# Attention followed by a gated FFT convolution on one core: a rewritten order of the first two batches, one hand-over per group of filter spectra, and output rows in fewer, larger transfers

## Chip, cores and metric

The kernel runs on one NeuronCore of a Trainium2 chip. The metric is the device time of one execution in microseconds. A run's span is the time from the first to the last instruction in the profile; the execution's own time is a little longer than its span.

## What is computed

Eight batches of 576 rows. A linear attention without softmax gives x (eight heads of 64 columns, side by side: 512 columns), and a gated long convolution follows:

```python
kv  = einsum('bhsd,bhse->bhde', k, v)
out = einsum('bhsd,bhde->bhse', q, kv)
x   = out / sqrt(mean(out*out, axis=-1) + 1e-6) * g_norm      # heads side by side
x1, x2, x3 = split(x @ w_proj, 3, axis=-1)
X2  = rfft(x2, n=576, axis=1);  H = rfft(filter_fft, n=576, axis=0)
y   = x1 * irfft(X2 * H, n=576, axis=1) * x3
result = y @ w_out                                             # (8, 576, 512), fp32
```

## The kernel before

All work is written as named steps, and three strings, FIRST, ROUND and LAST, give the order in which the steps are written. `do(words, r)` walks a string: a word stands for a step of batch r, each `+` adds one to the batch, each `-` takes one off. A step that was done already, or whose batch doesn't exist, is skipped. FIRST holds the set-up and most of the first two batches, ROUND is walked for r = 0 to 6, LAST closes batch 7. Nothing reorders the instructions later: each engine runs its own in the order written, and waits on semaphores for the others.

The steps of a batch are these. Lk, Lv and Lq load k, v and q; POOL issues them and they are turned into bf16 on the way (line 100). K makes the eight k-v products (line 313) and eK copies them to `kvblk`. Qt transposes q by a transfer that SP issues (line 333); for batches 0 and 1, T0 and T1 do it on PE (line 340). O multiplies (line 376); sq (ACT, line 386) squares; R sums the squares through a matrix of ones, `ind` (line 383); rs takes the reciprocal root (ACT, line 397); ob or ov scales by g_norm; x0 and x1 multiply (DVE, line 409), which completes x. The transform is done in matmuls. 576 = 3 x 192, so fr, fd and fa (DVE, lines 420 to 434) fold x into a sum and two differences with mirrored halves; rrM, rrT, abM and abT multiply the folded parts by the middle third of w_proj (lines 450 to 471); err, eab and eT bring them to bf16 (ACT, line 475); F0, F1 and F2 apply the tables of cosines. M0, M1 and M2 multiply by the filter's spectra (DVE, lines 511, 512, 527), A0 (POOL) and Av1 (DVE) add the products (line 518). Ga and Gb are the gates from the first and last third of w_proj (line 537), x1j and gj their evacuations (lines 543, 545). Io and I transform back (lines 561, 562), os, u, w and fin put the rows together and gate them (`yg`, line 582). U0, U2 and U4 are the output product (line 609), ot0, ot2 and ot4 copy it to an `ot` tile and send it out from SP. Batch 7 uses V0 to V3 (line 641) with smaller pieces, whose copies run on ACT (va) and DVE (vv).

The set-up: Z and Zi fill constants (Zi's identity and counters on POOL), Zt and An0 to An2 make the angles and `IV`, the table for the inverse transform; Act asks ACT for the table set with the reciprocal root. Tb0 to Tb2 transpose `IV` into the forward tables, Ff0 to Ff2 fold the filter (line 261), and H0 to H2 make its spectra `HH` and `HM`: six or twelve matmuls, then for each half an ACT copy with a scale (line 289) and a DVE step (line 290). Words such as W1_ put four matmuls on zeros (W0_: ten, line 79) in front of the next step that takes a PSUM buffer.

PSUM is four pairs of banks. `take` gives the pair that was freed longest ago in the written order, so the order also decides who waits for whom. `ot` tiles are three, taken in turn:

```python
def ot_tile():
    turn[0] += 1
    return buf("ot", turn[0] % 3, [P, 2, DM], FP32)
```

Row order: column block `blk` of 32 holds the rows t, t + 6, t + 12 and so on, with t = `t_of(blk)`, so a block of 32 goes out with a step of six rows. U0 and U2 send pairs of such blocks, four transfers of 128 KB each; U4 and each V send four transfers of 64 KB, one for each block (lines 629 and 648). V's transfers go half from SP and half from ACT (va) or POOL (vv).

The transfers issued by SP and ACT take eight semaphores in turn, and a transfer waits until the one that last used its semaphore has landed.

Of the kernel before, what the change touches and what calls it, by code (L numbers as in the profile page):

```python
# [9 lines left out]
FP32 = mybir.dt.float32  # L10
BF16 = mybir.dt.bfloat16
I32 = mybir.dt.int32
AF = mybir.ActivationFunctionType
# [3 lines left out]
MAGIC = 3.0 * (2.0 ** 22)  # L17


FIRST = """Z Lq Lf Zi Lka Act Zt Lva An0 An1 An2 Lvb W0_ T1 Zf T0 eTv0 eTv1 Tb0 Lkb Lq+ Lw2 Ff2 Ff0 Tb2 Ff1 W2_ Ka eKa W1_ Tb1 O1 sq1  # L20
ov1 O0 sq0 R0 rs0 W6_ R1 Kb eKb rs1 ov0 O2 sq2 ov2 W7_ O3 Lk+ R2 sq3 R3 rs2 x0 rs3 ov3 x1 Lv+ fr1 T0+ fr0 T1+ eTa0+
Lw1 eTa1+ H2 H0 rrM fd0 rrT fa0 fd1 err fa1 W8_ H1 F0 W9_ abM eab K+ M0 eK+ abT O2+ eT sq2+ O0+ F2 sq0+ F1 ob2+ Lw3
ob0+ O3+ M2 sq3+ Lwo ob3+ M1 R2+ Ga0 Lq++ rs2+ Ga1 R3+ R0+ x10 Gb0 x11 O1+ A0 Av1 rs3+ rs0+ g0 Gb1 sq1+ ob1+
Lk++ R1+ x1+ Ga3 Ga2 g1 Io01 rs1+ Gb3 x13 Lv++ x0+ fr+ x12 os01 I01 rrM+ rrT+ fd+ fa+ g3 err+ abT+ eT+ Io23
u01 os23 I23 abM+ F0+ eab+ Gb2 F2+ u23 M0+ F1+ g2 M1+ w23 fin23 w01 fin01 K++ Lk+++ Qt++ Lq+++ eK++ W12_ O2++"""

ROUND = """K++ Lk+++ x0+ Qt++ U0- Lq+++ x13 eK++ fd+ Io23 u01 O2++ fa+ Gb3 fr+ ot0- Lv+++ os23 I23 abM+ g3 sq2++ u23
ob2++ rrM+ eab+ abT+ rrT+ eT+ U4- O1++ w01 err+ ot4- sq1++ ob1++ O3++ sq3++ fin01 ob3++ F1+ U2- w23 fin23 F0+
ot2- M1+ Ga1+ x11+ F2+ Ga0+ M0+ Gb0+ x10+ A0+ R3++ M2+ O0++ Gb1+ g0+ R2++ rs3++ Ga2+ g1+ sq0++ Av1+ ob0++
rs2++ R0++ x1++ Gb2+ x12+ R1++ rs0++ rs1++ g2+ Ga3+ Io01+ os01+ I01+"""  # L30

LAST = """u01 Io23 x13 U0- I23 w01 U2- os23 u23 fin01 ot0- Gb3 w23 ot2- g3 fin23 V2 V1 U4 va2 vv1 V3 V0 ot4 vv3 va0"""


@with_exitstack
def kernel(
# [19 lines left out]
    NB = S // 32  # L56
# [4 lines left out]
    act, vec = nc.scalar, nc.vector  # L61
# [71 lines left out]
    step = {}  # L133
# [135 lines left out]
    def gen_h(g):  # L269
        ff = tmp['ff']  # L270
        hp = take("h")
        n = N1 if g == 0 else P
        for ri in range(2):
            for a in range(3):
                m = P if a < 2 else 32
                kw = dict(start=(a == 0), stop=(a == 2))
                if g < 2:
                    nc.tensor.matmul(hp[:n, ri], FW[:m, a, 2 * g + ri, 0:n], ff[:m, a, ri], **kw)
                else:
                    for dup in range(2):  # L280
                        nc.tensor.matmul(hp[dup * NM:(dup + 1) * NM, ri], FW[:m, a, 4 + ri, ri * NM:(ri + 1) * NM], ff[:m, a, ri], **kw)
        u = work.tile([P, 2, DM], FP32, name="hu", tag="ot%d" % g)
        if g < 2:
            todo = [(HH[:n, g, 1], 0, cf[:n, 0, g:g + 1], cf[:n, 1, g:g + 1]),
                    (HH[:n, g, 0], 1, cf[:n, 0, g:g + 1], cf[:n, 2, g:g + 1])]
        else:
            todo = [(HM[:, i], 0, pc[:, 2 * i:2 * i + 1], pc[:, 2 * i + 1:2 * i + 2]) for i in range(2)]
        for i, (o_, ri, c1, c2) in enumerate(todo):
            act.activation(out=u[:n, i], in_=hp[:n, ri], func=AF.Copy, scale=c1)
            vec.scalar_tensor_tensor(out=o_, in0=hp[:n, 1 - ri], scalar=c2, in1=u[:n, i], op0=ALU.mult, op1=ALU.add)  # L290
        free("h")
        if g < 2:
            act.activation(out=HH[:n, g, 2], in_=HH[:n, g, 0], func=AF.Copy, scale=-1.0)

    for g in range(3):
        step["H%d" % g] = lambda b, g=g: gen_h(g)
    for n_, (d_, s_) in dict(Lw1=(wp[:, :, 0:DM], moe_w_proj[:, 0:DM]), Lw2=(wp[:, :, DM:2 * DM], moe_w_proj[:, DM:2 * DM]),
                             Lw3=(wp[:, :, 2 * DM:D3], moe_w_proj[:, 2 * DM:D3]), Lwo=(wo, moe_w_out)).items():
# [62 lines left out]
    sq = lambda: buf("sq", 0, [P, NDC, S])  # L361
    osb = lambda: buf("o", 0, [P, NDC, S])
    rstd = lambda: buf("rstd", 0, [P, NDC, S])
# [229 lines left out]
    def o_rows(b, *blks):  # L593
        t0 = [t_of(x) for x in blks]
        two = [[(t0[1] - t0[0]) * DM, 2]] if len(t0) == 2 else []
        return bass.AP(tensor=out.tensor, offset=out.offset + (b * S + t0[0]) * DM, ap=[[6 * DM, 32]] + two + [[1, DM]])

    turn = [0]

    def ot_tile():  # L600
        turn[0] += 1
        return buf("ot", turn[0] % 3, [P, 2, DM], FP32)

# [5 lines left out]
                nc.tensor.matmul(pp[:, cc], ygt(b)[:, dc, c * P:(c + 1) * P], wo[:, dc], start=(dc == 0), stop=(dc == NDC - 1))  # L609

    def U_ev(b, c0):
        ot = ot_tile()
        act.copy(out=ot, in_=tmp['u', b, c0])  # L613
        free(("u", b, c0))
        for i in range(4):
            nc.sync.dma_start(out=o_rows(b, 4 * c0 + i, 4 * c0 + 4 + i), in_=ot[32 * i:32 * i + 32])
# [5 lines left out]
                nc.tensor.matmul(pp[64 * i:64 * i + 64], ygt(b - 1 + i)[:, dc, 4 * P:S], wo[:, dc], start=(dc == 0), stop=(dc == NDC - 1))  # L622

    def U4_ev(b):
        ot = ot_tile()
        act.copy(out=ot[:, 0], in_=tmp['u4', b])
        free(("u4", b))
        for i in range(4):
            nc.sync.dma_start(out=o_rows(b - 1 + i // 2, NB - 2 + i % 2), in_=ot[32 * i:32 * i + 32, 0])

    for c0 in (0, 2):
        step["U%d" % c0] = lambda b, c0=c0: U(b, c0)
        step["ot%d" % c0] = lambda b, c0=c0: U_ev(b, c0)
# [4 lines left out]
    def V(b, c):  # L638
        pp = tmp['u', b, c] = take(("u", b, c), 1)
        for dc in range(NDC):  # L640
            nc.tensor.matmul(pp, ygt(b)[:, dc, c * P:(c + 1) * P], wo[:, dc], start=(dc == 0), stop=(dc == NDC - 1))

    def V_ev(b, c, ev, q1):
        ot = ot_tile()
        ev(out=ot[:, 0], in_=tmp['u', b, c])
        free(("u", b, c))
        for i in range(4):
            (q1 if i >= 2 else nc.sync).dma_start(out=o_rows(b, 4 * c + i), in_=ot[32 * i:32 * i + 32, 0])

    for c in range(4):  # L650
        step["V%d" % c] = lambda b, c=c: V(b, c)
        step["va%d" % c] = lambda b, c=c: V_ev(b, c, act.copy, nc.scalar)
        step["vv%d" % c] = lambda b, c=c: V_ev(b, c, vec.tensor_copy, nc.gpsimd)


    did = set()
# [21 lines left out]
    do(LAST, B - 1)

# [29 lines left out]
```

## Time and profile before

| | |
|---|---|
| median of 3 runs | 231.14 us (230.54 to 233.3) |
| the profiled execution | 231.38 us, span 229.6 us |
| PE, DVE, ACT, POOL busy | 91%, 83%, 66%, 20% of the span |
| granted TensorE clock, mean | 0.974 |
| HBM | 33.69 MB read, 9.44 MB written |
| transfers to the output | 56 of 128 KB and 24 of 64 KB from SP, 4 of 64 KB each from ACT and POOL |

The first load is issued at 1.31 us and its first reader starts at 8.83 us. The output of batch 0 begins to leave at 81 us. In the lists below, a line such as L537 is a line of the kernel before, PE is the matmul engine, DVE, ACT and POOL are the vector, scalar and GpSimd engines, SP issues transfers. A busy share is a mean over stages that have different limits, so each stage has to be read by itself.

### The profile page before, as it was taken

How to read it: one execution, taken by the hardware profiler on the slowest of the kernel's cores; microseconds unless marked ns; L12 is line 12 of the kernel's file. 1: busy time of each engine (PE TensorE's matmuls, PEld its weight loads, DVE VectorE, ACT ScalarE, POOL GpSimd, SP SyncE). 2: the span in 40 equal slices, each digit the busy share in tenths (PEclk: the TensorE clock that was granted, in tenths of full speed). 3: DMA queues.
4: the chain of work that ended last, by engine and by line, in shares of the span. 5: the costliest groups of instructions: out<-in, count | busy, mean ns of one | idle time of the engine just before them, and what ended most of it. 6: DMA issues, size and time to landing. Idle time of an engine off the chain costs nothing.

```text
span 229.6 us, 4731 instructions
## 1 busy us (share of the span) xinstructions
PE 209.0 (91%) x1860; PEld 126.4 (55%) x1881; DVE 191.7 (83%) x323; ACT 152.3 (66%) x238; POOL 45.8 (20%) x55
## 2 busy tenths in 40 slices
PE   7397897899989999999999999999999999999770
PEld 2244433476547755775577557745774676467320
DVE  4864587789898999899889998998899989998920
ACT  7737866995468768776877688768776784533421
POOL 7751000550080000800080008000400040012030
PEclk9859999999999999999999999999999999999995
DMA  4999998599969630999299919993803120350464
GB/s 44 195 202 205 204 207 138 103 142 204 192 100 199 98 91 18 185 184 213 62 185 175 224 34 174 188 206 79 162 3 91 41 55 21 87 126 0 114 179 121
DMA packets 41193, 30.14 MB, mean 131 GB/s; under 512 B 16050, under 2 KB 36530, under 8 KB 41170
## 3 DMA queue, kind: packets, MB, share of 16 engines
q0 software_dynamic: 21200, 17.11, 49.3%
q1 hardware_dynamic: 19778, 12.46, 24.0%
q8 instruction: 15, 0.25, 0.4%
q10 hardware_dynamic: 192, 0.26, 0.4%
q14 instruction: 8, 0.07, 0.1%
HBM read 33.69 MB, written 9.44 MB: 188 GB/s over the span
## 4 chain that ended last, share of the span: by engine, by line
PE 72%; DVE 15%; ACT 6%; issue 2%; DMA 2%; POOL 1%; ACTq 0%; DVEq 0%; POOLq 0%
PE ps L537 26%; PE ps L609 9%; PE ps L464 5%; PE ps L561 4%; PE ps L383 3%; PE ps L471 3%; PE ps L450 3%; PE ps L313 2%; PE ps L376 2%; PE ps L261 2%; PE ps L505 2%; PE ps L497 2%; DMA out_dram<-ot 2%; PE ps L457 1%; PE ps L490 1%
## 5 line engine op out<-in xcount | busy, mean ns | idle before, releaser
L537 PE MATMUL ps<-x,wp 128*128 128x288 bf16 x512 | 71.3, 286 | 0.6 <-ACT o L393 0.5
L537 PEld LDWEIGHTS <-wp 128*128 128x128 bf16 x512 | 49.0, 98 | 17.1 <-issue 1.1
L518 POOL TENSOR_TENSOR Y<-tpw 97x1024 bf16<-97x1024 f32 x8 | 18.8, 2353 | 157.8 <-PE ps L537 79.3
L475 ACT CAST x<-ps 128x1024 bf16<-128x1024 f32 (+1 forms) x24 | 20.3, 871 | 16.3 <-PE ps L464 8.9
L543 ACT CAST x<-ps 128x576 bf16<-128x576 f32 x32 | 20.5, 644 | 12.5 <-PE ps L537 12.0
L545 DVE TENSOR_TENSOR g<-ps,x 128x576 bf16<-128x576 f32 x32 | 24.0, 754 | 5.3 <-PE ps L537 5.1
L609 PE MATMUL ps<-wo,yg 128*128 128x512 bf16 x105 | 26.1, 380 | 0.4
L397 ACT ACTIVATE rstd<-ps,bias_eps 128x576 bf16<-128x576 f32 x32 | 23.6, 745 | 4.2 <-PE ps L383 3.3
L386 ACT ACTIVATE sq<-ps 128x576 bf16<-128x576 f32 x32 | 21.0, 662 | 1.7 <-PE ps L376 1.7
L511 DVE TENSOR_TENSOR tpw<-ps,HH 97x1024 f32<-97x1024 f32 (+1 forms) x16 | 19.5, 1220 | 2.0 <-PE ps L498 1.3
L393 ACT ACTIVATE o<-ps,g_col 128x576 bf16<-128x576 f32 x28 | 21.1, 758 | 0.0
L512 DVE TENSOR_TENSOR tpw<-ps,HH 97x1024 f32<-97x1024 f32 (+1 forms) x16 | 19.4, 1215 | 0.0
L613 ACT COPY ot<-ps 128x1024 f32<-128x1024 f32 x14 | 14.3, 1022 | 7.5 <-PE ps L609 7.4
L609 PEld LDWEIGHTS <-yg 128*128 128x128 bf16 x112 | 10.4, 98 | 11.6
L561 PE MATMUL ps<-IV,Y 128*128 128x192 bf16 x128 | 16.2, 245 | 0.0
L464 PE MATMUL ps<-wp,ab 128*128 128x512 bf16 x64 | 15.1, 379 | 0.0
L565 ACT COPY os<-ps 128x576 f32<-128x576 f32 x16 | 10.3, 642 | 7.1 <-PE ps L562 6.1
L383 PE MATMUL ps<-sq,ind 128*128 128x288 bf16 x64 | 12.9, 286 | 1.9 <-ACT sq L386 1.6
L570 DVE TENSOR_TENSOR u<-ps,os 128x576 bf16<-128x576 f32 x16 | 12.0, 750 | 1.8 <-ACT os L565 1.8
L409 DVE TENSOR_TENSOR x<-o,rstd 128x1152 bf16<-128x1152 bf16 x16 | 12.1, 755 | 1.4 <-ACT rstd L397 1.3
L562 PE MATMUL ps<-IV,Y 97*128 97x96 bf16 x64 | 13.2, 207 | 0.0
L79 PE MATMUL ps<-kvblk,ind 128*128 128x512 bf16 x35 | 11.5, 452 | 1.8 <-DVE ind L145 1.6
(137 smaller groups left out, 339.0 us busy)
## 6 DMA issues: line engine op xcount, KB each, us to landing
out_dram<-ot SPq DMA_DIRECT2D x56, 128.0 KB, 2.4
qb<-in_q_dram POOLq DMA_DIRECT2D x8, 576.0 KB, 9.7
kb<-in_k_dram POOLq DMA_DIRECT2D x7, 576.0 KB, 7.1
vb<-in_v_dram POOLq DMA_DIRECT2D x7, 576.0 KB, 11.7
wp<-in_moe_w_proj_dram POOLq DMA_DIRECT2D x3, 512.0 KB, 18.2
out_dram<-ot SPq DMA_DIRECT2D x24, 64.0 KB, 1.7
fn<-in_moe_filter_fft_dram POOLq DMA_DIRECT2D x1, 576.0 KB, 9.3
kb<-in_k_dram POOLq DMA_DIRECT2D x2, 288.0 KB, 9.5
```

Of the source, the lines that this page charges most:

```text
L383: nc.tensor.matmul(r2[:, h, 0:TH], ind, sq()[:, j, h * TH:(h + 1) * TH], start=True, stop=True)
L386: act.activation(out=halves(sq()[:, j]), in_=tmp['o', b, j][:, :, 0:TH], func=AF.Square)
L393: act.activation(out=by_time(osb(), j), in_=i_, func=AF.Copy, scale=g_col)
L397: act.activation(out=by_time(rstd(), j), in_=by_row(tmp['r', b, j]), func=AF.Abs_reciprocal_sqrt, scale=1.0 / D, bias=bias_eps)
L464: nc.tensor.matmul(pp[:, h], abt()[:, j, h * SB:h * SB + P], w2(j), start=(j == 0), stop=(j == NDC - 1))
L475: act.copy(out=o_(), in_=tmp[key, b])
L511: vec.tensor_mul(out=t_[:n, 0], in0=xp[:n], in1=HH[:n, g, 1:3])
L537: nc.tensor.matmul(pp[:, h, 0:TH], w_, x[:, j, h * TH:(h + 1) * TH], start=(j == 0), stop=(j == NDC - 1))
L543: act.copy(out=x1, in_=pp[:, :, 0:TH])
L545: vec.tensor_mul(out=halves(g13t()[:, dc]), in0=pp[:, :, 0:TH], in1=x1)
L561: nc.tensor.matmul(pp[:, i, 0:SB], Y[:, 2 * g + h, cs], IV[:, 2 * g + h, 0:SB], start=(g == 1), stop=(g == 2))
L609: nc.tensor.matmul(pp[:, cc], ygt(b)[:, dc, c * P:(c + 1) * P], wo[:, dc], start=(dc == 0), stop=(dc == NDC - 1))
```

## The change

The three strings are written anew. Zi comes ahead of the first load, the filter's load comes after K and V of batch 0, w1 is loaded before w2, q of batch 2 before k and v of batch 1. Act stands behind the last angles. Of the eight words that put warm matmuls, W0_ and W1_ stay (10 and 4 matmuls; before, 38 in all). Loads and transposes of q are written one batch further ahead, and FIRST reaches further into batches 1 to 3.

```diff
-FIRST = """Z Lq Lf Zi Lka Act Zt Lva An0 An1 An2 Lvb W0_ T1 Zf T0 eTv0 eTv1 Tb0 Lkb Lq+ Lw2 Ff2 Ff0 Tb2 Ff1 W2_ Ka eKa W1_ Tb1 O1 sq1
-ov1 O0 sq0 R0 rs0 W6_ R1 Kb eKb rs1 ov0 O2 sq2 ov2 W7_ O3 Lk+ R2 sq3 R3 rs2 x0 rs3 ov3 x1 Lv+ fr1 T0+ fr0 T1+ eTa0+
-Lw1 eTa1+ H2 H0 rrM fd0 rrT fa0 fd1 err fa1 W8_ H1 F0 W9_ abM eab K+ M0 eK+ abT O2+ eT sq2+ O0+ F2 sq0+ F1 ob2+ Lw3
...
+FIRST = """Zi Lq Z Lka Zt An0 An1 An2 Lva Act Lkb W0_ Lvb Lf T0 T1 Zf eTv0 eTv1 Tb0 Tb2 Ka eKa Tb1 Kb O1 sq1 O0 sq0 eKb
+W1_ R1 Lq+ ov1 rs1 O3 R0 sq3 ov0 rs0 ov3 Ff1 R3 Lw1 O2 x0 rs3 fd0 sq2 Lw2 Ff2 Ff0 T0+ R2 fa0 Lq++ rs2 ov2 x1
+fr1 eTa0+ H0 Ga1 fd1 fa1 fr0 Lv+ H2 x11 H1 abM rrM rrT abT err eT T1+ Lk+ eab eTa1+ F0 Qt++ K+ eK+ Ga0 F2 M0
+O3+ O2+ x10 F1 sq3+ Lw3 M2 sq2+ O1+ ob3+ ob2+ M1 Gb1 O0+ sq1+ ob1+ Lk++ R3+ Gb0 sq0+ g1 rs3+ Lv++ Lwo R2+ A0
+R0+ Av1 ob0+ Io01 g0 rs2+ R1+ rs0+ rs1+ K++ os01 I01 x1+ Ga2 x0+ Io23 eK++ O3++ x12 sq3++ u01 os23 fr+ Ga3 Gb3
...
+ROUND = """Ga3 O2++ ot0- Lq++++ x13 sq2++ ob2++ fa+ fr+ Gb3 g3 abM+ Lk+++ I23 w01 rrM+ abT+ rrT+ Qt+++ eab+ u23 eT+ U4-
+err+ O3++ O1++ ot4- sq1++ F1+ sq3++ ob1++ Lv++++ ob3++ fin01 U2- F0+ w23 M1+ Ga0+ ot2- R3++ x10+ rs3++ M0+
+Av1+ Ga1+ F2+ x11+ R2++ rs2++ R1++ rs1++ M2+ Gb0+ Gb1+ O0++ Ga2+ sq0++ g0+ R0++ g1+ ob0++ K+++ rs0++ x12+
+eK+++ A0+ Gb2+ fin23 Io01+ x1++ x0++ os01+ g2+ I01+ fd++ u01+ U0 Io23+ os23+"""
+LAST = """I23 ot0- w01 Ga3 u23 x13 fin01 U2- Gb3 w23 g3 fin23 U4 ot2- ot4 V2 V0 va2 V1 V3 va0 vv1 vv3"""
```

The spectra: for groups 0 and 1 one ACT copy takes both halves, and the DVE steps follow.

```diff
+        if g < 2:
+            act.activation(out=u[:n], in_=hp[:n], func=AF.Copy, scale=todo[0][2])
+        else:
+            for i in range(2):
+                act.activation(out=u[:n, i], in_=hp[:n, 0], func=AF.Copy, scale=todo[i][2])
         for i, (o_, ri, c1, c2) in enumerate(todo):
-            act.activation(out=u[:n, i], in_=hp[:n, ri], func=AF.Copy, scale=c1)
             vec.scalar_tensor_tensor(out=o_, in0=hp[:n, 1 - ri], scalar=c2, in1=u[:n, i], op0=ALU.mult, op1=ALU.add)
```

The output: neighbouring blocks whose rows start two rows apart go out in one transfer, with a DRAM pattern of `k` groups of 32 rows. For the last two batches every second `ot` tile is one of three attention tiles that are no longer needed.

```diff
+    def o_runs(b, c, n):
+        runs, i = [], 0
+        while i < n:
+            k = 1
+            while i + k < n and t_of(4 * c + i + k) == t_of(4 * c + i) + 2 * k:
+                k += 1
+            step_ = [[2 * DM, k]] if k > 1 else []
+            runs.append((i, k, bass.AP(tensor=out.tensor, offset=out.offset + (b * S + t_of(4 * c + i)) * DM,
+                                       ap=step_ + [[6 * DM, 32], [1, DM]])))
+            i += k
+        return runs
...
+    def ot_tile(b):
+        if b >= B - 2:
+            turn[1] += 1
+            if turn[1] % 2:
+                t = (sq, osb, rstd)[turn[1] // 2 % 3]()
+                return t.rearrange("p a b -> p (a b)").bitcast(FP32)[:, 0:2 * DM].rearrange("p (a b) -> p a b", a=2)
         turn[0] += 1
...
     def U4_ev(b):
-        for i in range(4):
-            nc.sync.dma_start(out=o_rows(b - 1 + i // 2, NB - 2 + i % 2), in_=ot[32 * i:32 * i + 32, 0])
+        for i in range(2):
+            for p, k, where in o_runs(b - 1 + i, 4, 2):
+                nc.sync.dma_start(out=where, in_=ot[64 * i + 32 * p:64 * i + 32 * (p + k), 0])
...
     def V_ev(b, c, ev):
-        for i in range(4):
-            (q1 if i >= 2 else nc.sync).dma_start(out=o_rows(b, 4 * c + i), in_=ot[32 * i:32 * i + 32, 0])
+        for q1, (p, k, where) in zip((nc.sync, nc.scalar), o_runs(b, c, 4)):
+            q1.dma_start(out=where, in_=ot[32 * p:32 * (p + k), 0])
```

With `t_of` this gives V0 and V3 a transfer of 96 rows (k = 3) on SP and one of 32 on ACT, V2 one of 32 on SP and one of 96 on ACT, V1 two of 64 (k = 2), and U4 two of 64 on SP. U0 and U2 are sent as before.

## Prediction, written before the changed kernel ran

> **What bounds the kernel now.** I read the page first, then the chain of waits in order of time, then windows cut at the places where the chain repeats itself.
>
> ```profile
> span 229.6 us, 4731 instructions
> ...
> PE 209.0 (91%) x1860; PEld 126.4 (55%) x1881; DVE 191.7 (83%) x323; ACT 152.3 (66%) x238; POOL 45.8 (20%) x55
> ```
> ```profile
> 77.36 0.88 PE ps L313 x48
> ...
> 87.60 1.73 PE ps L609 x8
> ...
> 89.98 0.98 PE ps L537 x8
> 90.96 0.65 PE ps L505 x3
> ...
> 99.66 0.88 PE ps L313 x48
> ...
> 122.82 0.88 PE ps L313 x48
> ```
> ```profile
> core 0: us, PE busy (x) PEld busy (x) DVE busy (x) ACT busy (x) POOL busy (x), PEclk, DMA share, GB/s
> 77.36:99.66 22.30, 22.20 (x213) 14.14 (x216) 21.05 (x32) 16.63 (x27) 4.61 (x4) 1.00 0.48 92
> 99.66:122.82 23.16, 23.05 (x221) 14.58 (x224) 21.23 (x32) 17.22 (x28) 4.63 (x4) 1.00 0.91 159
> 49.00:77.36 28.36, 27.09 (x257) 17.99 (x259) 25.05 (x38) 19.09 (x32) 4.61 (x4) 1.00 1.18 178
> 10.00:25.00 15.00, 12.31 (x137) 6.40 (x136) 8.34 (x34) 9.15 (x16) 3.81 (x5) 0.78 1.27 200
> ```
>
> The 91% is a mean over three stages. From 77 us to about 212 us the same round comes back every 22.30 us (23.16 us with U4), PE is busy for 22.20 us of it, and DVE for 21.05 us (94%). That stage is PE's, and the change leaves its matmuls as they are, so a new order can't shorten a round; it can only lengthen one. What can move is the start (to about 49 us), where PE waits on loads and on the DVE and ACT hand-overs, the 1.27 us of PE idle time between 49 and 77 us, and the tail behind the last yg.
>
> ```profile
> 217.50 0.76 DVE L582 TENSOR_TENSOR yg<-w,g 128x1152 bf16<-128x1152 bf16 x1
> ...
> 218.96 0.58 ACT L645 COPY ot<-ps 128x512 f32<-128x512 f32 x1 [2.86 <-PE ps L641]
> ...
> 219.58 0.86 ACTq L648 DMA_DIRECT2D out_dram<-ot  x2
> ...
> 223.91 0.58 ACT L645 COPY ot<-ps 128x512 f32<-128x512 f32 x1 [2.51 <-DMA out_dram<-ot]
> ...
> 225.27 1.83 SPq L648 DMA_DIRECT2D out_dram<-ot  x4
> ```
>
> The last yg ends at 218.27; call it T. From T to the end of the span are 11.3 us: five evacuations, 20 transfers of 64 KB on three queues, and one copy that waits 2.51 us for its ot buffer.
>
> **The start.** Twenty-four of the 38 warm matmuls go, the loads are written in another order (Zi's POOL work ahead of the first load, the filter behind K and V), the reload of ACT's table goes, and the spectra take one ACT copy of 1024 columns where there were two of 512.
>
> ```profile
> 1.31 0.92 POOL L100 DMA_DIRECT2D qb<-in_q_dram  x1 [0.87 <-POOLq L693]
> ...
> 2.73 0.23 POOL masks.py:197 MEMSET ident<- 128x128 bf16 x1
> ...
> 4.61 0.71 POOL L100 DMA_DIRECT2D kb<-in_k_dram  x1
> ...
> 8.83 1.43 PE L340 MATMUL ps<-ident,qb 96*128 96x96 bf16 x24 [2.77 <-DMA qb<-in_q_dram]
> ...
> 18.30 0.57 PE L313 MATMUL ps<-vb,kb 96*64 96x64 bf16 x24
> ...
> 21.91 1.28 ACT L397 ACT_TABLE_LOAD   x1
> ...
> 23.38 0.57 PE L313 MATMUL ps<-vb,kb 96*64 96x64 bf16 x24
> ...
> 28.50 0.76 DVE L409 TENSOR_TENSOR x<-o,rstd 128x1152 bf16<-128x1152 bf16 x1
> ...
> 35.21 0.75 DVE L290 SCALAR_TENSOR_TENSOR HH<-ps,cf,hu 97x512 f32<-97x512 f32 x1 [0.76 <-ACT hu L289]
> ...
> 39.65 0.75 DVE L290 SCALAR_TENSOR_TENSOR HH<-ps,cf,hu 128x512 f32<-128x512 f32 x1 [0.75 <-ACT hu L289]
> ...
> 40.91 0.95 PE L313 MATMUL ps<-vb,kb 96*64 96x64 bf16 x48
> ...
> 47.87 1.22 DVE L518 TENSOR_TENSOR Y<-tpw 128x1024 bf16<-128x1024 f32 x1
> ```
>
> Loads. At 200 GB/s (the window 10 to 25) a full q, k or v (96x8x384 bf16, 0.59 MB) takes 2.9 us, a third of w_proj (0.52 MB) 2.6 us. Zi takes 1.9 us of POOL (2.73 to 4.61), now ahead of the first load, so q lands at 8.83 + 1.9 = 10.7. Behind it K and V in four halves of 1.45: 16.5. Filter 19.4, q of batch 1 22.3, w1 24.9, w2 27.5, q of batch 2 30.4, v1 33.3, k1 36.2, w3 38.8. By the same sum k0 and v0 are complete at 17.5 in the kernel before, and v1 at 28.8: the first attention can begin a microsecond earlier, the second K not before 36.2.
>
> Attention of batch 0. Before, its two K halves stood at 18.30 and 23.38, behind fold and warm matmuls, and a table load of 1.28 stood between sq and rs. Now both K halves run as they land (done by 17.1), and ACT's list from there is two kvblk copies (0.5), four sq at 0.62, four rs at 0.70 and two filter evacuations at 1.0: 7.8 us, so the last rs is at about 25.3 and x is complete at 26.1; before, 29.26. Gain 3.2 us.
>
> Spectra. Before, ACT and DVE answered each other in turn, each DVE step behind its own ACT copy (0.76 idle, 0.75 work), up to 40.4. Now DVE's list from 25.3 is x (0.77), fr, fd and fa for half a batch and fr for the other (1.2, 0.55, 0.63, 1.2) and six spectra steps at 0.75: 8.9 us, done at 34.2. The longer copy isn't seen: the row below gives it 1.02 against two times 0.69.
>
> ```profile
> L613 ACT COPY ot<-ps 128x1024 f32<-128x1024 f32 x14 | 14.3, 1022 | 7.5 <-PE ps L609 7.4
> ```
>
> What is late next is k1 at 36.2. Queued behind K+ on PE are Ga0, F2, O3+, O2+ and F1; at 0.9, 0.98, 0.65, two times 0.37 and 0.86 they end at 40.3. DVE then has M1 (2.35), g1 (0.7) and Av1 (1.15), and ends Av1 at 44.6, against 49.09 before: 4.5 us earlier. PE has by then Gb1 and O1+ behind it as well, which before ended at about 51.1; by that measure it is 6.5 us. I take **5.0 us earlier**. Bounds: 8 us, if the 1.27 us of idle time and the last four warm matmuls (0.9) are saved too; nothing, if the later loads and new stalls in the rounds (six rounds, 0.3 us each, DVE being at 94%) eat it. With 24 warm matmuls less nothing else is lost in the sum, since PE waits there for loads or ACT.
>
> **The tail.** Its row groups change shape. Before, every address pattern of the output had an outer count of 32 or more. Now V0, V2 and V3 send one of 96 rows, whose address pattern in DRAM is 3 groups of 32 rows, and one of 32 rows; V1 sends two of 64 rows (2 groups of 32), U4 two of those. The trace has one transfer of that shape, g_col, 2 groups of 64.
>
> ```profile
> q1 hardware_dynamic: 130, 0.00, 1.1%
> ...
> g_col<-in_g_norm_dram SPq DMA_DIRECT2D x1, 0.5 KB
> ```
> ```profile
> q10 hardware_dynamic: 192, 0.26, 8.3%
> ```
> ```profile
> GB/s 273 242 270 280 294 328 379 389 287 359 331 406 410 365 420 328 393 355 284 273 239 202 147 164 109 300 82 55 82 55 27 27 27 27 27 27 0 0 0 0
> ...
> q1 hardware_dynamic: 318, 0.52, 46.2%
> ```
> ```profile
> out_dram<-ot SPq DMA_DIRECT2D x24, 64.0 KB, 1.7
> ```
>
> The first row is the DMA view of 0 to 5 us, when g_col is alone on its queue: 128 elements and only 2 packets more. The second is ACT's queue from 219 to 230 us: four transfers of 32 packets of 2 KB, and 64 packets more, 16 for each. So the small extra packets count the DMA engines that a transfer runs on: 16 where the outer count is 32, 2 where it is 2. I conclude that the 64-row transfers run on 2 engines and the 96-row ones on 3, with 32 packets of 2 KB on each. The trace doesn't name engines; I take the same first ones each time. Then engine 0 carries V0, V1 twice, V2, V3 and U4 twice, 7 x 32 = 224 packets, and 6 more of the 32-row transfers. A packet's price: from 152 to 155 us the queue's 256 data packets took 46.2% of 16 x 3.0 us, 22.2 us, so 85 ns; in ACT's row, with others beside them, 8.3% of 16 x 11 us, 14.6 us over 128, at most 114 ns. I take 85, since two or three engines leave the others idle. 230 x 0.085 = 19.5 us.
>
> From T: the rest of U4 and V2 (eight matmuls at 0.22, 1.8), V2's copy (0.6), and 1.5 us until packets move (1.7 to landing less two packets), so engine 0 starts at 3.5 and, being fed without a break, ends at 23.0. The span closes 1.2 us after the last landing (225.27 + 1.83 - 0.43 + 1.7 = 228.4, span 229.6): T + 24.2 against T + 11.3, **12.9 us more**. SP's order doesn't hide it: by the eight semaphores taken in turn, U4's first transfer waits for V2's 96-row one on ACT, and V0, V1 and V3 are queued behind it on SP. Six buffers do take away the wait of 2.51. Bounds with the shared engine: 78 ns a packet (420 GB/s over 16, the highest slice of that view) gives 11.3 more, 110 ns (ACT's row less its small packets) 18.7 more.
>
> The Trainium skill (DMA: Bandwidth & Descriptors, "Why a DMA increments its semaphore by 16 and not by 1") has the same as a rule: the number of engines is the largest up to 16 that divides the slowest dimension of both address patterns, so 2 and 3 here, and a transfer from SP or ACT uses the lowest-numbered ones. g_col's 130 packets agree with the first half; no run so far shows the second; by it the tail would also be 12.9 us longer.
>
> Mid-run U4 (three times) puts 64 packets, 5.4 us, on two engines. The loads beside it are wanted more than 10 us later, so it costs nothing; with that cover gone, up to 5.4 us each.
>
> **Sum**, against the profiled execution's own 231.38 (its span and 1.8 us around it; the median of the runs shown is 231.14): 231.4 - 5.0 + 12.9 = **239.3 us**.
>
> **Rivals.** (1) Few engines, but others for each transfer. Then each takes 2.7 us by itself, and the chain of SP's waits decides: V2's on ACT lands at T + 6.4, V0 follows, V1 waits for its ACT half (about 8.4), V3 is issued at 9 and lands at 13.2: T + 14.4, 3.1 more. 231.4 - 5.0 + 3.1 = 229.5. For it: no row names an engine. (2) On the other side: the shape doesn't matter for large rows and every transfer runs on 16 engines. Then 10 transfers instead of 20 and no buffer wait give about T + 9.8, 1.5 less: 224.9, faster. It decides if more than about 8 engines carry each thin transfer. Against it: g_col's 2. (3) The clock. PE's granted clock was 0.78 from 10 to 25 us even with the warm matmuls. If it stays at half until 30 us, some 7 us of PE work there takes twice as long, half of it in waits: 3.5 of the 5.0 are lost, 242.8.
>
> The Trainium skill (TensorE: Matmul & The Clock Gate, Part 1) holds that an idle window of about 3.4 us halves PE's clock and a busy one restores it. The 0.78 agrees with that; it is what would make rival 3.
>
> **How the numbers follow.** The sum as forecast 0.68, rival 1 0.10, rival 2 0.10, rival 3 or stalls in the rounds 0.12. The likeliest one's own range is 234 to 246 (start 0 to 8 us, tail 11.3 to 18.7, both ends seldom together); to leave out no more than 2 in 10 I reach down to rival 1: 228.5 to 246. About 2% is what a measurement of this kernel tells from no change, 226.5 to 235.8. Rival 2 and a little of 1 lie below: 0.10. Rival 1 and the forecast with a start better than 8 us lie within: 0.20. Slower: 0.70.
>
> **What would show it.** Thin transfers right: the extra packets of ACT's queue at the end are 3 + 16 + 2 + 16 = 37, not 64; DMA share in the last 15 us is about 0.15 to 0.2; the span ends over 20 us after the last yg. Wrong: 64 of them, or a high share and an end 10 us after. The start is right if Av1 of batch 0 ends at 43 to 46 us and x of batch 0 is complete by 27; wrong if K+ waits past 38 or the clock is at half beyond 25 us. Rounds of 22.3 and 23.2 us show the middle unchanged.

## The result and the profile after

The changed kernel takes 240.16 us (median, 238.71 to 240.59) against 231.56 us (230.54 to 233.3) on the same chip: ratio 1.035, 95% interval 1.027 to 1.043. It is slower. The profiled execution took 240.24 us. All ratios here leave out the slow executions, those more than 1.5% above the fastest of their kernel.

The page's first lines, and the timeline around the last yg:

```profile
span 238.5 us, 4646 instructions
...
PE 205.3 (86%) x1833; PEld 125.1 (52%) x1857; DVE 190.4 (80%) x323; ACT 148.6 (62%) x234; POOL 48.9 (21%) x51
```
```profile
211.30 0.76 DVE L589 TENSOR_TENSOR yg<-w,g 128x1152 bf16<-128x1152 bf16 x1
214.36 1.36 ACTq L674 DMA_DIRECT2D out_dram<-ot  x1
...
216.43 0.37 ACTq L674 DMA_DIRECT2D out_dram<-rstd  x1
216.90 0.57 ACTq L674 DMA_DIRECT2D out_dram<-ot  x1
217.56 0.41 ACTq L674 DMA_DIRECT2D out_dram<-sq  x1
220.43 1.22 SPq L655 DMA_DIRECT2D out_dram<-o  x2
221.75 0.42 SPq L674 DMA_DIRECT2D out_dram<-ot  x1
222.27 0.79 SPq L674 DMA_DIRECT2D out_dram<-rstd  x1
223.16 1.15 SPq L674 DMA_DIRECT2D out_dram<-ot  x1
224.41 1.45 SPq L674 DMA_DIRECT2D out_dram<-sq  x1
```

The last yg ends at 212.06, T from here on; before, T was 218.27. From T to the end of the span are 26.4 us, before 11.3. So the time splits into two parts of opposite sign: 6.2 us less up to T, 15.1 us more behind it. The last matmul has long ended when SP issues its last transfer at 224.41, and the span runs on for another 14 us.

What those 14 us are, three views show: the windows, the transfers from 214 us on, and SP's waits at the very end.

```profile
core 0: us, PE busy (x) PEld busy (x) DVE busy (x) ACT busy (x) POOL busy (x), PEclk, DMA share, GB/s
114.41:136.72 22.31, 22.06 (x212) 13.99 (x216) 20.97 (x32) 16.53 (x27) 5.15 (x4) 1.00 0.90 155
136.72:159.89 23.17, 22.92 (x219) 14.46 (x224) 20.96 (x32) 17.12 (x27) 3.18 (x1) 1.00 0.55 109
...
220.00:225.00 5.00, 0.00 (x0) 0.00 (x0) 0.00 (x0) 0.00 (x0) 0.00 (x0) 0.50 0.19 59
225.00:230.00 5.00, 0.00 (x0) 0.00 (x0) 0.00 (x0) 0.00 (x0) 0.00 (x0) 0.50 0.18 52
230.00:235.00 5.00, 0.00 (x0) 0.00 (x0) 0.00 (x0) 0.00 (x0) 0.00 (x0) 0.50 0.17 67
```
```profile
q1 hardware_dynamic: 444, 0.85, 10.6%
q10 hardware_dynamic: 261, 0.46, 7.2%
```
```profile
SPq L655 <- DMA out_dram<-ot: 7.8, 1, 7.8
SPq L730 <- DMA out_dram<-o: 3.5, 1, 3.5
SPq L730 <- DMA out_dram<-ot: 2.5, 1, 2.5
SPq L730 <- DMA out_dram<-sq: 2.5, 1, 2.5
SPq L730 <- DMA out_dram<-rstd: 2.5, 1, 2.5
```

No engine computes from 220 us on. The DMA share of 0.17 to 0.19 is 2.7 to 3.0 of 16 engines. ACT's queue has 261 packets: 224 of data (96 + 32 + 64 + 32 rows) and 37 more, 3 + 16 + 2 + 16. And the last transfers, issued a microsecond apart, land 2.5 us apart: 32 packets at about 0.08 us, one transfer behind the other on the same engine. The rounds in the middle are as long as before (22.31 and 23.17 us).

The start, with the lines that answer to the prediction's:

```profile
14.48 0.85 PE L320 MATMUL ps<-vb,kb 96*64 96x64 bf16 x24
...
24.01 0.76 DVE L416 TENSOR_TENSOR x<-o,rstd 128x1152 bf16<-128x1152 bf16 x1
...
31.31 1.40 DVE L297 SCALAR_TENSOR_TENSOR HH<-ps,cf,hu 128x512 f32<-128x512 f32 x2
35.20 0.95 PE L320 MATMUL ps<-vb,kb 96*64 96x64 bf16 x48
42.50 1.22 DVE L525 TENSOR_TENSOR Y<-tpw 128x1024 bf16<-128x1024 f32 x1
```
```profile
45.00:47.00 2.00, 0.00 (x0) 0.00 (x0) 0.96 (x2) 1.21 (x3) 0.00 (x0) 1.00 1.26 207
47.00:49.00 2.00, 1.81 (x56) 1.70 (x57) 0.00 (x0) 0.79 (x3) 0.57 (x1) 0.81 1.28 202
49.00:51.00 2.00, 2.00 (x11) 1.37 (x10) 1.93 (x4) 0.37 (x2) 1.72 (x3) 0.50 1.31 203
51.00:53.00 2.00, 2.00 (x20) 1.41 (x18) 1.97 (x4) 1.55 (x3) 0.00 (x0) 0.84 1.31 203
```
```profile
PE ps L320 <- DMA vb<-in_v_dram: 2.3, 1, 2.3
```

x of batch 0 is complete at 24.77 (before 29.26), the spectra at 32.71 (40.40), Av1 ends at 43.72 (49.09). Then comes a wait that is new: K of batch 2 stands until 47.19 for the load of v (the last row, from PE's waits). PE does nothing from 45 to 47 us, and its granted clock is 0.50 from 49 to 51.

### The profile page after: what moved, and what is told of

Its sections match the earlier page's. It is cut to its first block, busy times and chain, and to the rows that moved or that the text cites. A ratio compares the mean times of both kernels' runs of the same rounds, so it can differ in the third digit from the quotient of the medians.

```text
span 238.5 us, 4646 instructions
## 1 busy us (share of the span) xinstructions
PE 205.3 (86%) x1833; PEld 125.1 (52%) x1857; DVE 190.4 (80%) x323; ACT 148.6 (62%) x234; POOL 48.9 (21%) x51
## 4 chain that ended last, share of the span: by engine, by line
PE 68%; DMA 17%; POOL 2%; DVE 2%; issue 1%; ACT 0%; DVEq 0%; POOLq 0%
PE ps L544 25%; DMA vb<-in_v_dram 11%; PE ps L634 10%; DMA qb<-in_q_dram 6%; PE ps L471 5%; PE ps L568 4%; PE ps L478 3%; PE ps L390 3%; PE ps L383 2%; PE ps L320 2%; PE ps L457 2%; PE ps L512 2%; PE ps L504 2%; PE ps L667 1%; PE ps L647 1%; PE ps L464 1%
## 5 line engine op out<-in xcount | busy, mean ns | idle before, releaser
L544 PEld LDWEIGHTS <-wp 128*128 128x128 bf16 x512 | 48.6, 98 | 15.7 <-issue 0.7
L525 POOL TENSOR_TENSOR Y<-tpw 97x1024 bf16<-97x1024 f32 x8 | 23.8, 2974 | 130.8 <-DVE tpw L519 112.5
L552 DVE TENSOR_TENSOR g<-ps,x 128x576 bf16<-128x576 f32 x32 | 23.9, 752 | 3.5 <-PE ps L544 3.0
L634 PE MATMUL ps<-wo,yg 128*128 128x512 bf16 x106 | 26.1, 379 | 0.3
L393 ACT ACTIVATE sq<-ps 128x576 bf16<-128x576 f32 x32 | 20.4, 665 | 9.3 <-PE ps L383 9.3
L404 ACT ACTIVATE rstd<-ps,bias_eps 128x576 bf16<-128x576 f32 x32 | 23.0, 741 | 3.0 <-PE ps L390 2.8
L400 ACT ACTIVATE o<-ps,g_col 128x576 bf16<-128x576 f32 x28 | 20.4, 758 | 0.0
L572 ACT COPY os<-ps 128x576 f32<-128x576 f32 x16 | 10.2, 640 | 15.1 <-DVE u L578 10.7
L568 PE MATMUL ps<-IV,Y 128*128 128x192 bf16 x128 | 17.1, 251 | 0.0
L638 ACT COPY ot<-ps 128x1024 f32<-128x1024 f32 x13 | 13.3, 1024 | 4.5 <-PE ps L634 4.5
L471 PE MATMUL ps<-wp,ab 128*128 128x512 bf16 x63 | 15.1, 379 | 0.1
L577 DVE TENSOR_TENSOR u<-ps,os 128x576 bf16<-128x576 f32 x16 | 12.1, 753 | 2.8 <-PE ps L569 2.8
L416 DVE TENSOR_TENSOR x<-o,rstd 128x1152 bf16<-128x1152 bf16 x16 | 12.1, 755 | 1.8 <-ACT rstd L404 1.6
L568 PEld LDWEIGHTS <-Y 128*128 128x128 bf16 x128 | 10.7, 100 | 3.8 <-DVE Y L525 0.2
L390 PE MATMUL ps<-sq,ind 128*128 128x288 bf16 x64 | 12.1, 286 | 0.4 <-DVE tpw L519 0.4
```

The lines of the kernel that those rows point to most:

```text
L393: act.activation(out=halves(sq()[:, j]), in_=tmp['o', b, j][:, :, 0:TH], func=AF.Square)
L400: act.activation(out=by_time(osb(), j), in_=i_, func=AF.Copy, scale=g_col)
L404: act.activation(out=by_time(rstd(), j), in_=by_row(tmp['r', b, j]), func=AF.Abs_reciprocal_sqrt, scale=1.0 / D, bias=bias_eps)
L471: nc.tensor.matmul(pp[:, h], abt()[:, j, h * SB:h * SB + P], w2(j), start=(j == 0), stop=(j == NDC - 1))
L525: op(out=Yt()[:n, 2 * g:2 * g + 2], in0=t_[:n, :, 0], in1=t_[:n, :, 1])
L544: nc.tensor.matmul(pp[:, h, 0:TH], w_, x[:, j, h * TH:(h + 1) * TH], start=(j == 0), stop=(j == NDC - 1))
```

## The experiments

**Undoing the shape of the transfers.** Theory S: the thin transfers share the lowest engines. Four kernels change the shape alone. In e1_wide both U4 and V send 32 rows a transfer again (V's first two on SP, the others on ACT), in e3_u4_wide U4 alone, in e4_v_wide V alone; e2_thin_before puts the thin transfers into the kernel before.

```diff
 # e1 (both), e3 (U4 alone), e4 (V alone), on the changed kernel; e2 the other way round, on the kernel before
 U4_ev:
-        for i in range(2):
-            for p, k, where in o_runs(b - 1 + i, 4, 2):
-                nc.sync.dma_start(out=where, in_=ot[64 * i + 32 * p:64 * i + 32 * (p + k), 0])
+        for i in range(4):
+            nc.sync.dma_start(out=o_rows(b - 1 + i // 2, NB - 2 + i % 2), in_=ot[32 * i:32 * i + 32, 0])
 V_ev:
-        for q1, (p, k, where) in zip((nc.sync, nc.scalar), o_runs(b, c, 4)):
-            q1.dma_start(out=where, in_=ot[32 * p:32 * (p + k), 0])
+        for i in range(4):
+            (nc.scalar if i >= 2 else nc.sync).dma_start(out=o_rows(b, 4 * c + i), in_=ot[32 * i:32 * i + 32, 0])
```

> The changed kernel, but U4 and V send 32 rows a transfer again (20 transfers of 64 KB behind the last yg, SP and ACT in halves); order and six buffers stay. Theory S (thin transfers all share the lowest two or three engines): the tail falls from 26.4 us behind the last yg to about 9.8, the last yg stays at 212; 240.2 - 16.6 = 223.6, 222 to 226. Rival O (not the shape but the order of the queues sets the tail: U4 behind V2's half on ACT, V0, V1 and V3 behind U4): twice as many transfers in the same order, not under 236.

> The kernel before with one thing changed: U4 and V send runs of 64 or 96 rows in one transfer. Three buffers, the old order. Theory S: the last yg stays at 218.3 and the same 230 packets of 2 KB go through one engine behind it, 13 to 15 us more: 245 to 247. Rival O (the new order and the buffers make the tail long): fewer issues, so 230 to 233.

> The changed kernel with U4 alone in 32-row transfers; V stays thin. Theory S: the first engine loses 64 packets and gets 8, 56 x 0.085 to 0.092 us = 4.8 to 5.2 us less: about 235. Rival D (each thin transfer is on few engines, but on others than the one before, and the chain of waits between transfers sets the tail): U4 is out of the chain only with what it takes by itself beside V, under 1 us less: 239 to 240.2.

> The changed kernel with V alone in 32-row transfers; U4 stays thin, two transfers of 64 rows. Theory S: the first engine has U4's 64 packets and 2 for each of V's 16 transfers, some 100 instead of 230; 130 x 0.085 to 0.092 = 11 to 12 us less: 228 to 229, or less where V's packets go past U4's. Rival D: two thin transfers on different engines, 2.7 us each and beside V: as with all of them wide, 223 to 225.

| kernel | us (median, range) | ratio to before, 95% | T to end of span |
|---|---|---|---|
| e1_wide | 227.31 (225.75 to 228.34) | 0.979 (0.971 to 0.988) | 13.4 |
| e2_thin_before | 248.03 (246.55 to 250.39) | 1.068 (1.058 to 1.078) | 25.1 |
| e3_u4_wide | 237.58 (236.28 to 239.23) | 1.025 (1.017 to 1.033) | 23.9 |
| e4_v_wide | 230.16 (228.77 to 231.99) | 0.994 (0.989 to 0.998) | 16.6 |

The shape is the whole loss. Put right, the changed kernel is 12.9 us faster than it was; put into the kernel before, it costs 15.7 us by the ratio (13.4 to 17.9), where 13 to 15 were expected. Rival O (the order of the queues alone) is out by e1 and e2: it wanted 236 or more, and 230 to 233. Rival D (few engines, but others each time) is out by e4: D wanted 223 to 225, and all ten runs are above 228.7. e3 points the same way: taking U4's 64 packets from the thin ones brings 2.6 us, where D allowed under 1; but the intervals of the two ratios overlap, so e3 alone doesn't settle it. The profiled execution of e2 was a late one (T at 222.2); two of its copies wait 5.3 and 10.3 us for one of the three `ot` buffers, which the thin transfers hold.

S had the direction right, but all four medians lie above its ranges: e1 227.3 for 222 to 226, e2 248.0 for 245 to 247, e3 237.6 for about 235, e4 230.2 for 228 to 229. In e1, e3 and e4 SP's queue has a part in it. e1 was to end 9.8 us behind T and ended 13.4 behind. Its timeline and SP's waits:

```profile
214.72 0.85 ACTq L673 DMA_DIRECT2D out_dram<-ot  x2
216.29 0.80 ACTq L673 DMA_DIRECT2D out_dram<-rstd  x2
217.18 0.86 ACTq L673 DMA_DIRECT2D out_dram<-ot  x2
217.98 1.74 SPq L654 DMA_DIRECT2D out_dram<-o  x4
...
222.63 0.84 SPq L673 DMA_DIRECT2D out_dram<-sq  x2
```
```profile
SPq L654 <- DMA out_dram<-rstd: 4.7, 1, 4.7
```

U4's copy ends at 213.7, but its first transfer goes out at 217.98, because its semaphore is still held by a transfer of ACT's from `rstd`; eight more issues of 0.43 us stand behind U4's four. U4 is written ahead of the V steps and still waits for one of theirs, so the semaphores were not dealt out in the written order. In e4 this wait is 4.6 us. In e3 it is 7.9 us (U4 issued at 220.82), as it is in the changed kernel, and the first 96-row transfer of SP goes out at 223.75, 11.3 us behind T where the changed kernel has 10.2. So of the 4.8 us that U4's packets are worth there, 1.1 are given back as time in which SP has nothing on the shared engine. The tail of e3 is 2.5 us shorter; where the rest went is not shown.

**The tail without that wait.** e8_pairs copies V2 and V3 into one buffer and V0 and V1 into another, and sends each as four transfers of 32 rows x 2 (128 KB), the shape that U0 and U2 have; nothing is left on ACT's queue.

```diff
 # e8, on e1
-LAST: ... V2 V0 va2 V1 V3 va0 vv1 vv3
+LAST: ... V2 V0 V3 V1 va2 va0 vv3 vv1
 V_ev:
-        ot = ot_tile(b)
-        ev(out=ot[:, 0], in_=tmp['u', b, c])
+        c0 = c // 2 * 2
+        if c % 2 == 0:
+            tmp['vo', c0] = ot_tile(b)
+        ot = tmp['vo', c0]
+        ev(out=ot[:, c - c0], in_=tmp['u', b, c])
...
-        for i in range(4):
-            (nc.scalar if i >= 2 else nc.sync).dma_start(out=o_rows(b, 4 * c + i), in_=ot[32 * i:32 * i + 32, 0])
+        if c % 2:
+            for i in range(4):
+                (nc.gpsimd if i == 3 else nc.sync).dma_start(out=o_rows(b, 4 * c0 + i, 4 * c0 + 4 + i), in_=ot[32 * i:32 * i + 32])
```

> On the kernel of the wide transfers, the last batch's V2 and V3, and V0 and V1, are copied into one buffer each and leave in four transfers of 32 rows x 2 (128 KB), three on SP and one on POOL: 12 transfers behind the last yg instead of 20, none on ACT, so that none of SP's waits for one of ACT's. Theory Q (with 16 engines the tail of 13.4 us is SP's issues of 0.44 us behind a wait of 4.7 us for a transfer of ACT): U4 at 213.7, last issue at 219.3, landing 2.4 later, span 222.5 to 223.5, time 224 to 225. Rival L (the bytes or the landing set it): not under 226.5.

224.44 us (223.68 to 224.96), ratio 0.969 (0.962 to 0.976), T to end 11.5 us. SP's issues behind the last yg in this kernel:

```profile
212.98 1.74 SPq L654 DMA_DIRECT2D out_dram<-o  x4
...
215.87 1.27 SPq L677 DMA_DIRECT2D out_dram<-ot  x3
...
217.26 2.72 SPq L677 DMA_DIRECT2D out_dram<-rstd  x3
```

U4 now goes out 0.6 us after its copy begins, and theory Q gives the time. The next run, e12_pairs_again, is the base of e9, e10 and e11.

> The kernel of the pairs (e8) once more, as the base of this comparison: 223.7 to 225.5 whichever theory holds; last yg between 210.4 and 212.4, later where the granted clock falls to half behind the 2.3 us in which PE waits for v of batch 2.

It is not quite the kernel of e8, as was expected of it, and neither are e9, e10 and e11, which are built on it: they send two of each four transfers from ACT.

```diff
 # e12, e9, e10 and e11, against e8
-                (nc.gpsimd if i == 3 else nc.sync).dma_start(out=o_rows(b, 4 * c0 + i, 4 * c0 + 4 + i), in_=ot[32 * i:32 * i + 32])
+                (nc.scalar if i >= 2 else nc.sync).dma_start(out=o_rows(b, 4 * c0 + i, 4 * c0 + 4 + i), in_=ot[32 * i:32 * i + 32])
```

e12 takes 226.04 us (224.87 to 227.53), above the 223.7 to 225.5 expected; its ratio of 0.974 (0.968 to 0.981) overlaps with e8's. In the profiled executions T is 0.8 us later than in e8 (212.49 against 211.66). The end is 12.1 us behind T against 11.5, and U4's transfers wait for one of ACT's again:

```profile
SPq L654 <- DMA out_dram<-ot: 4.2, 1, 4.2
```

So of the 1.9 us by which e8's tail is shorter than e1's, 1.3 come with the pairs even when ACT sends half of them, and 0.6 with taking ACT out.

**What made the start shorter.** The prediction put it on the first attention and on the spectra's handover. The two were undone one at a time: e5_two_copies (on e1) and e11_pairs_two (on e12) have the two ACT copies in turn with DVE, e10_filter_early (on e12) loads the filter ahead of k and v of batch 0; e6_before_one_copy gives the kernel before the single copy.

```diff
 # e5, e11; e6 the other way round, on the kernel before
-        if g < 2:
-            act.activation(out=u[:n], in_=hp[:n], func=AF.Copy, scale=todo[0][2])
-        else:
-            for i in range(2):
-                act.activation(out=u[:n, i], in_=hp[:n, 0], func=AF.Copy, scale=todo[i][2])
         for i, (o_, ri, c1, c2) in enumerate(todo):
+            act.activation(out=u[:n, i], in_=hp[:n, ri], func=AF.Copy, scale=c1)
 # e10
-FIRST = """Zi Lq Z Lka Zt An0 An1 An2 Lva Act Lkb W0_ Lvb Lf T0 ...
+FIRST = """Zi Lq Z Lf Lka Zt An0 An1 An2 Lva Act Lkb W0_ Lvb T0 ...
```

> On the kernel of the wide transfers (e1: 227.3 us, last yg ends at 212.4), the filter spectra take their two ACT copies in turn with DVE again. Theory C (the loads set the start: K of batch 1 waits for its k at about 35 whatever the spectra do): the spectra end some 4 us later, at about 37, still before F1 and M1 need them; last yg within 0.5 us of 212.4, time 227 to 228. Rival H (the handovers were on the path, as the prediction had it for the kernel before): up to six waits of 0.75 us come back, last yg 3 to 4.5 us later, 230 to 232.

> The kernel before with the one ACT copy for each group of the spectra, nothing else. Rival H: in the old order DVE waits for ACT up to 40.4 us, so 2 to 4 us of it go: last yg at 214.5 to 216.5 instead of 218.3, time 227.5 to 229.5. Theory C (the order of the loads and the first attention, not this copy, made the start shorter): within 1 us of 231.5.

> On the pairs (e8), the filter is loaded ahead of k and v of batch 0 again, as in the kernel before. The sum of the loads up to k of batch 1 stays, only k0 and v0 land 2.9 us later. Theory C (the loads' sum sets the start: k of batch 1 at 35, v of batch 2 at 47): x of batch 0 2 to 3 us later, K of batch 1 and the last yg within 1 us; 224 to 225.5. Rival A (the attention of batch 0 is on the path, 3.2 us as in the prediction): last yg 2.5 to 3.2 us later, 227 to 227.6.

> On the pairs (e8), the spectra in two copies in turn. Theory C (covered by the wait for loads): the spectra end 2 to 3 us later, PE's work slides into its wait at 45 to 47.5, last yg within 0.5 us; 224 to 225. Rival H (the longer handover is paid): 226 or more.

| kernel | us (median, range) | ratio to before, 95% | x of batch 0 | Av1 ends | T |
|---|---|---|---|---|---|
| e5_two_copies | 226.14 (225.56 to 226.41) | 0.977 (0.971 to 0.983) | 24.77 | 46.28 | 210.78 |
| e6_before_one_copy | 230.38 (229.5 to 231.43) | 0.994 (0.991 to 0.998) | 29.24 | 47.91 | 217.07 |
| e12_pairs_again (base) | 226.04 (224.87 to 227.53) | 0.974 (0.968 to 0.981) | 25.21 | 44.47 | 212.49 |
| e10_filter_early | 225.55 (225.41 to 226.11) | 0.974 (0.969 to 0.978) | 28.16 | 47.11 | 211.60 |
| e11_pairs_two | 225.03 (224.6 to 225.69) | 0.971 (0.966 to 0.976) | 25.17 | 46.69 | 211.19 |

Neither is paid for. With the filter early, x of batch 0 comes 2.95 us later and Av1 2.6 us later, and T is not later at all; with two copies Av1 comes 2.2 us later, and again T is not. Rivals A and H, which are the prediction's own two gains, wanted 227 and 226 us or more, and over a base of 226.04 still more. A part of the base's late T is its clock, of which more below; but against e8, with T at 211.66, e10 and e11 aren't later either. K of batch 1 does start later, at 38.49 in e10 against 36.21, more than the 1 us that theory C allowed, and T doesn't follow it. T of e5 is earlier than theory C had it (210.78 for 212.4), at a clock of 1.00 where e1's fell to 0.50. In the old order the one copy is worth 1.3 us by the ratio (0.5 to 2.2), not the 2 to 4 that rival H expected.

The windows say why. This is 45 to 51 us, first of the base e12, then of e11:

```profile
45.00:47.00 2.00, 0.60 (x7) 0.29 (x4) 1.30 (x3) 2.00 (x4) 0.00 (x0) 1.00 1.25 201
47.00:49.00 2.00, 1.35 (x55) 1.33 (x56) 0.36 (x1) 0.46 (x2) 0.10 (x1) 1.00 1.27 204
49.00:51.00 2.00, 2.00 (x15) 1.39 (x13) 1.76 (x3) 0.87 (x4) 2.00 (x3) 0.57 1.31 203
```
```profile
45.00:47.00 2.00, 2.00 (x17) 1.47 (x17) 2.00 (x3) 2.00 (x4) 0.00 (x0) 1.00 1.26 200
47.00:49.00 2.00, 1.98 (x61) 1.60 (x59) 1.43 (x3) 2.00 (x4) 0.00 (x1) 1.00 1.28 212
49.00:51.00 2.00, 1.89 (x23) 1.46 (x21) 2.00 (x4) 1.84 (x6) 2.00 (x3) 1.00 1.31 199
```

In the base PE runs ahead until 45 us and then stands for v of batch 2 until 47.65; in e11 it comes to the same step at 47.75 and has nothing to wait for. In both rows of 45 to 47 the loads run at 200 GB/s. Work that comes later merely fills that wait, and the clock stays at 1.00 where the base falls to 0.57. By these rows T is set by the loads up to v of batch 2 and by PE's work; no run made the loads fewer, so that is a reading and not a test.

What PE had to do changed by the warm matmuls. The windows 8 to 50 us of before and after:

```profile
8.00:50.00 42.00, 35.82 (x351) 18.51 (x355) 28.83 (x69) 30.60 (x51) 11.73 (x14) 0.92 1.07 173
```
```profile
8.00:50.00 42.00, 37.00 (x408) 21.10 (x412) 31.00 (x71) 32.14 (x52) 12.03 (x15) 0.98 1.27 201
```

PE is busy 1.2 us more after the change. Of the warm matmuls, the ten of W0_ run from 1.61 to 6.06 us in both kernels, ahead of these windows; the others take 6.1 us of the window before and 1.6 us after. So PE spends 5.7 us more on the kernel's own work by 50 us. Not all of that is more work, because the clock was at half for a part of it. Before, that part is 9.6 to 16.5 us. After, the trace has no clock record ahead of 17.5 us, and the row's 0.98 counts that time as full; but K's 24 matmuls at 14.48 take 0.85 us, as in e12 at a clock of 0.50, where the kernel before takes 0.57 at 18.30 at a clock of 1.00. So the clock was at half there too, and I take it as half from 8 to 17.5 us. With busy time at half clock counted half, the lead by 50 us is 4.2 us. From there to T come 1.0 us for the last warm matmuls and 1.4 us less of PE's idle time, and 0.8 us are lost to the half clock up to 51.7: 5.8 us in all, against the 6.2 at T. The loads, at 201 GB/s where they were at 173, let it. This accounting is read from the traces; no kernel was run with the warm matmuls put back, nor one with the old table reload.

**Filling the wait for v of batch 2.** K of batch 2 is written later, so that other matmuls stand in front of it: behind I01, Ga2 and Io23 in e7_k2_later (on e1), behind I01 and Ga2 in e9_pairs_k2 (on e12).

```diff
-... rs1+ K++ os01 I01 x1+ Ga2 x0+ Io23 eK++ O3++ ...
+... rs1+ os01 I01 x1+ Ga2 x0+ Io23 K++ eK++ O3++ ...    # e7
+... rs1+ os01 I01 x1+ Ga2 K++ x0+ Io23 eK++ O3++ ...    # e9
```

> On the kernel of the wide transfers, K of batch 2 is written behind I01, Ga2 and Io23 instead of ahead of them (3 us of matmuls), so that PE has work while v of batch 2 lands. Theory W (PE idles 2.3 us for that load at 45 to 47.5 and the middle is PE's): last yg 1.5 to 2.3 us earlier, 225 to 226. Rival V (DVE and ACT are behind there anyway and the wait only moves to O of batch 2): within 0.5 us of 227.3.

> On the pairs (e8), K of batch 2 is written behind I01 and Ga2, with Io23 left behind it to cover the copies of kvblk. Theory W (PE's wait for v of batch 2 at 45 to 47.5 is lost time of the middle): 1.6 us of work goes into it, last yg 0.7 to 1.6 us earlier, and the clock does not fall to half at 49; 223 to 223.7. Rival V (only moved; the middle catches up or DVE is the bound): 224.2 to 225.

e7: 225.85 us (225.58 to 227.13), 0.977 (0.971 to 0.983), beside e1's 0.979: not told apart. T is 212.02 against e1's 212.43, not the 1.5 to 2.3 us earlier of theory W, and PE now waits 1.2 us for the copies of `kvblk`. e9: 224.92 us (224.19 to 226.25), ratio 0.971 (0.965 to 0.976), beside its base e12 with 0.974 (0.968 to 0.981). T is 211.09 against 212.49, within the 0.7 to 1.6 us that theory W wanted; but against e8, whose clock stayed at 1.00, it is only 0.6 us, the time is in rival V's range (224.2 to 225) and not in W's (223 to 223.7), and the medians are 1.1 us apart with overlapping intervals. As a gain in time this stays unproven. The wait itself is shown to shrink. PE's waits in e9:

```profile
PE ps L383 <- ACT kvblk L326: 0.7, 1, 0.7
PE ps L320 <- DMA vb<-in_v_dram: 0.6, 1, 0.6
```

Of the 2.1 to 2.4 us for v 0.6 are left, and 0.7 come back as a wait for the copies of `kvblk`. e8, e9 and e11 are the best here, 2.9 to 3.1% under the kernel before and 6 to 7% under the changed one.

## Why the prediction was right

It said 239.3 us, slower, and for the reason that the runs show; it was right as a whole, and partly by two errors of opposite sign.

- **The tail** (forecast +12.9, bounds 11.3 to 18.7; measured +15.1). The mechanism holds in each of its signs: 37 extra packets on ACT's queue, a share of 0.17 to 0.19 in the last 15 us, an end 26.4 us behind the last yg. U4's first transfer waits 7.8 us for V2's on ACT, as the prediction had it from the eight semaphores. Mis-sized was the price of a packet: 19.5 us for 230 packets were 85 ns each, and from T + 3.6 to T + 24.9 they take 21.3 us, 93 ns. In the steady stretches a packet does take 84 ns; the rest is lost in two stretches (215 to 217 and 225 to 228), where the first 96-row transfers of ACT and of SP begin and single packets of the trace take up to 0.8 us; the windows above have 52 GB/s from 225 to 230 us and 67 from 230 to 235. e3 has two such stretches as well. Why a thin transfer begins slowly is open. The Trainium skill (DMA: Bandwidth & Descriptors, "Why a DMA increments its semaphore by 16 and not by 1") says that the transfers of SP and ACT use the lowest-numbered engines; before the change no row showed it, and now the landings 2.5 us apart and e4 agree.
- **The start** (forecast 5.0, bounds 0 to 8; measured 6.2). Every milestone came in the order forecast and about a microsecond early: x of batch 0 at 24.77 (forecast 26.1), spectra 32.7 (34.2), K of batch 1 35.2 (36.2), Av1 43.7 (44.6). A part of it is q, which was forecast at 10.7 and is read at 8.55: Zi's 1.9 us of POOL did not push it back. But the "Gain 3.2 us" for the attention and the shorter handovers of the spectra were not what T gained, as e10 and e11 show; the forecast came near, partly by luck, because the point that it measured from, k of batch 1 at 36, was set by the same sum of loads. That sum, which ends with w3 at 38.8, should have been carried two loads further, to v of batch 2, where PE stands for 2.3 us: 44.6 by the prediction's 2.9 us a load. PE has it at 47.19. From 30 to 48 us the transfer that transposes q of batch 2 moves another 0.59 MB beside the loads, out of the same 196 GB/s; with 2.9 us for it the sum gives 47.5.
- **The middle** was unchanged, as said.
- **Rival 2** (16 engines whatever the shape) is out by the 37 extra packets. That e8, with 16 engines, runs in 224.4 and the rival said 224.9 is luck: T came 6.6 us earlier where it took 5.0, and the tail was 11.5 us where it took 9.8. **Rival 1** is out by e4. **Rival 3** had the clock at half until 30 us. In e12 it is at 0.50 and 0.64 from 10 to 20 us, and by the length of its matmuls it was no faster in the changed kernel; still K of batch 1 waits 0.6 us for its load in e12: a slow clock that early is covered by the loads. From 25 to 30 us it was at 1.00 in every profiled execution. What does show at T is the half clock behind the wait at 47 us.

## What to carry to other kernels

Fewer and larger transfers are no gain in themselves: read from the extra packets of a queue on how many engines one runs, and keep an outermost count in its address pattern that spreads it: 32 gave 16 engines here, 3 and 2 gave 3 and 2; where two blocks are to go together, keep the 32 rows outside and put the pair inside, as e8 does. When a start-up is reordered, sum the loads up to the last one that PE must have: what is saved ahead of that load was not saved here. Count in it what other queues move meanwhile. And when transfers of two queues take semaphores in turn, a long one on the first queue holds up the second.

## What was not expected of the hardware

The same wait of PE for v of batch 2 is followed by a granted clock near one half in some executions and not in others of the same order: 0.50 from 49 to 51 us in the changed kernel (2.3 us of waiting) and in e1 (2.3 us), 0.53 in e3 (1.8 us), 0.57 in e12 (2.1 us), but 1.00 throughout in e8 (2.4 us) and in e4 (1.1 us).

```profile
45.00:47.00 2.00, 0.30 (x2) 0.00 (x0) 1.43 (x2) 1.67 (x3) 0.00 (x0) 1.00 1.30 204
47.00:49.00 2.00, 1.34 (x55) 1.33 (x56) 0.00 (x0) 0.36 (x1) 0.10 (x1) 1.00 1.24 195
49.00:51.00 2.00, 1.89 (x22) 1.44 (x20) 1.76 (x3) 1.49 (x5) 2.00 (x3) 1.00 1.31 203
```

These are e8's windows. The clock records of the traces suggest why. In each of the 14 profiled executions all changes of the clock lie on a grid with cells of 3.41 us, and the grid lies elsewhere in each execution: its first boundary is 0.45 us behind the start of the span in the changed kernel and 1.82 us in e8. The cell in which PE waits seems to decide the clock of the next one:

| run | cell, us | PE busy in it, us | clock in the next cell |
|---|---|---|---|
| after | 44.82 to 48.24 | 1.07 | half |
| e1_wide | 45.27 to 48.68 | 1.13 | half |
| e12_pairs_again | 45.87 to 49.29 | 1.64 | half |
| e3_u4_wide | 44.06 to 47.48 | 1.72 | half |
| e7_k2_later | 33.21 to 36.62 | 1.91 | half |
| e8_pairs | 46.19 to 49.60 | 1.94 | full |
| e9_pairs_k2 | 46.46 to 49.88 | 2.29 | full |
| e4_v_wide | 44.27 to 47.68 | 2.31 | full |

In the changed kernel the wait lies in one cell; in e8 a boundary cuts it in two, and the cell ahead still has 2.50 us of work. The limit isn't sharp in PE's busy time: in e2 a cell with 2.12 us (35.94 to 39.35) was followed by half the clock too. No run was made to move the wait within the grid. The Trainium skill (TensorE: Matmul & The Clock Gate, Part 1) has a window of about 3.4 us of idling before the clock halves; here the length agrees, but 1.3 us (e2) to 2.3 us (the changed kernel) of idle time within such a cell were enough. T is at 212.1 to 212.5 us in the four executions with the half clock behind 47 us whose code is the same up to there, and at 211.7 (e8) and 210.4 (e4) in the two without.
